# Cosine attention into a hard-swish MLP: the attention output of two pairs through one transposing DMA

## The chip, the cores and the metric

One core of a Trainium2 chip. The time is device microseconds of one execution of the program; a kernel's time is the median over its runs. In the text and in the profile PE is the matmul engine (PEld its weight loads), DVE the vector engine, ACT the scalar engine, POOL the general-purpose engine, and SP the engine that does nothing here but issue DMAs, one after another in program order.

## What is computed

Eight batches of twelve heads, 448 tokens, head dimension 64; the tokens then go through a two-layer MLP with a gated activation (768 to 2048 to 768). Inputs and output are float32.

```python
q_n = q / (np.linalg.norm(q, axis=-1, keepdims=True) + 1e-06)
k_n = k / (np.linalg.norm(k, axis=-1, keepdims=True) + 1e-06)
scores = np.matmul(q_n, k_n.transpose(0, 1, 3, 2)) / tau
attn = softmax(scores)                      # over the last axis
attn_out = np.matmul(attn, v)
x = attn_out.transpose(0, 2, 1, 3).reshape(B * S, H * D)      # 3584 x 768
h = x @ w_in
out = (h * np.clip(h + 3.0, 0.0, 6.0) / 6.0) @ w_out
```

## The kernel before

**Pairs and batches.** Two heads make a pair, so there are 48 pairs, numbered i = 0 to 47, six to a batch: pair i belongs to batch i // 6. For a pair, PE computes scores (L394), ACT their exponentials (L412), PE the product with v (L433), all in small groups; DVE then divides by the row sums and writes the pair's output as bf16 into a tile `on` of 128 x 512 (L448, L449, in `finish_values`). `on` has tokens on the partitions. The first matmul of the MLP needs the model dimension on the partitions, so `on` has to be transposed into `xT`: one 128 x 512 block of `xT[batch % 2]` for each pair.

**The way back.** For most of the first twelve pairs PE does this transpose (L466, L468) and DVE copies it out of PSUM (steps BK and CX). From pair 4 on, with few exceptions, SP does it with one transposing DMA of 128 x 512 elements (`back_crossbar`, L480, step XB): 42 of them. The tiles `on` come from a pool of three buffers, so the output of pair i can be written once the transpose of pair i - 3 has read its buffer.

**The MLP.** A batch's MLP starts when all its six pairs are in `xT`. It comes in units: `mm1_unit` (L496) is six matmuls of 448 columns over the six blocks of `xT`, block by block, so the k-th matmul reads the k-th pair of the batch; ACT (L505) and DVE (L511) turn its result into `gT`. `mm2_unit` (L532) is 16 matmuls over `gT` and ends in a copy (L543 on ACT or L545 on DVE) and two stores to the output (L553), which SP issues. The units of batch b are spread over the pairs of batch b + 1, so that PE always has matmuls beside the attention of the next pairs. Every engine works through its own list in program order.

**The order.** For the first 18 pairs the order of all steps is written out by hand in the strings of `PLAN`: two letters for the step, then the pair and other numbers. The steps that matter here: FI is `finish_values`, XB `back_crossbar`, VA the product with v, SC scores, EX exponentials, U one unit, UA and UV its work on ACT and DVE, LQ and LV loads of q or k and of v (issued on SP; L174 and L186), XD the transposing DMA of 128 x 896 elements that brings normalised q or k into place (L302, tile `tT`), CK and CS the copies of k (CS on POOL into `km`, L351), NM the normalising product (L246). From pair 18 on a loop (L682 to L722) gives the order. Its turn i does, in this order: SC i (three groups), EX i, VA i - 1, FI i - 1, the last group of SC and EX, then XB i - 1, for even i XD i + 2, one unit, some steps that prepare later pairs, one more unit, the other units of this turn, later preparations (for even i XD i + 3), LQ i + 7, for odd i LV, and VA i, group 0.

The first unit that reads a new batch b stands in turn i = 6 (b + 1) + 1, that is i = 19, 25, 31, 37, 43. The pair that completes the batch is transposed by the XB of the turn before. All DMA issues share SP's list with it: the loads, the stores (which wait for ACT's or DVE's copy) and the XDs.

Of the kernel before, what the change touches and what calls it, by code (L numbers as in the profile page):

```python
# [8 lines left out]
FP32 = mybir.dt.float32  # L9
BF16 = mybir.dt.bfloat16  # L10
AF = mybir.ActivationFunctionType
# [26 lines left out]
    "UA UA VA.7.0 EX.7.3 VA.7.1 UA CS.9.v UV W CS.8.v CK.8.v SC.8.0 UV UV SC.8.1 NM.10.p VA.7.2 VA.7.3 FI.7 EX.8.0",  # L38
    "SC.8.2 LQ.12 VC.8.p W EX.8.1 TR.10 U LV.5 EX.8.2 UA VA.8.0 CQ.11.v SC.8.3 SQ.13.p.0.7 VA.8.1 CQ.10.v UV",
    "SC.9.0 SC.9.1 EX.8.3 NM.11.p EX.9.0 RE.13 VA.8.2 SC.9.2 VA.8.3 FI.8 EX.9.1 SC.9.3 LQ.15 EX.9.2 U UA TR.11",  # L40
    "SQ.12.p.0.7 EX.9.3 RE.12 CS.11.v VA.9.0 VA.9.1 VC.10.p U CK.10.v XB.6 NO.6 NM.12.p VC.11.p SQ.15.p.0.7",
    "CK.11.v SC.10.0 CS.10.v UV VA.9.2 U UA SC.10.1 EX.10.0 UV UA EX.10.1 SC.10.2 VA.9.3 EX.10.2 LV.6 U UV UA",
    "TR.12 LQ.17 LQ.16 CQ.12.v XB.7 SC.10.3 U SQ.14.p.0.7 NM.13.p UV CQ.13.v SC.11.0 UA RE.15 FI.9 EX.10.3 EX.11.0",
    "U U UV UA UA VA.10.0 SC.11.1 EX.11.1 UV SC.11.2 EX.11.2 VA.10.1 UV VA.10.2 TR.13 SC.11.3 LQ.19 U LV.7 CS.12.a",
    "UA VA.10.3 RE.14 NO.7 SQ.17.p.0.7 NM.15.p CS.13.v CK.13.a U U FI.10 EX.11.3 UA VA.11.0 VA.11.1 VA.11.2",
    "NM.14.p SQ.16.a.0.7 UA CK.12.v SC.12.0 RE.17 XB.8 UV W U VA.11.3 VC.12.p U UV UV EX.12.0 FI.11 SC.12.1 UA",
    "XB.9 UV VC.15.p UA UV EX.12.1 LQ.18 SC.12.2 XB.10 VA.12.0 BK.11 SC.12.3 SC.13.0 EX.12.2 CX.11.v VA.12.1 XD.15",
    "U EX.12.3 EX.13.0 SC.13.1 SC.13.2 UA W U EX.13.1 VA.12.2 RE.16 SQ.19.p.0.7 VC.13.a VA.12.3 EX.13.2 UV SC.13.3",
    "UA U XD.14 FI.12 NO.8 UV SQ.18.p.0.7 CK.14.v U U EX.13.3 U VA.13.0 UA UV SC.14.0 UA UA UA EX.14.0 UV CS.14.v",
    "VC.14.a UV UV SC.14.1 EX.14.1 U SC.14.2 UA NM.16.v RE.19 UV EX.14.2 VA.13.1 U UA U W VA.13.2 UA RE.18 UV UV",  # L50
    "CK.15.v U LQ.20 SC.14.3 UA NO.9 XD.16 UV LQ.21 VA.13.3 U FI.13 U U NM.17.p XD.17 XB.13 UA VA.14.0 UV VA.14.1",
    "SC.15.0 UA EX.14.3 XB.12 VA.14.2 LV.8 UV UA UV EX.15.0 VA.14.3 SC.15.1 W EX.15.1 SC.15.2 FI.14 SQ.21.a.0.7",
    "CK.16.v EX.15.2 SC.15.3 SQ.20.a.0.2 U EX.15.3 U VA.15.0 SQ.20.p.2.5 VA.15.1 NM.19.v RE.20 UV SC.16.0 VC.17.v",
    "CS.16.v SC.16.1 UA CK.17.v SC.16.2 XD.19 EX.16.0 VC.16.v VA.15.2 RE.21 LQ.22 VA.15.3 U EX.16.1 EX.16.2",
    "SC.16.3 FI.15 UA NM.18.p U UV U XD.18 EX.16.3 UA NO.10 VA.16.0 VA.16.1 SC.17.0 SQ.22.p.0.7 SC.17.1 LV.9",
    "VC.18.p UV CK.18.v RE.22 EX.17.0 SC.17.2 VA.16.2 NM.20.v LV.11 XB.14 EX.17.1 VA.16.3 U LQ.23 VC.19.a SC.17.3",
    "UA U EX.17.2 FI.16 XB.16 UV CK.19.v LV.10 CS.18.v EX.17.3 VA.17.0 XB.15",
]


# [1 line left out]
def kernel(  # L62
# [10 lines left out]
    nc = tc.nc  # L73
    B, H, S, D = q.shape
# [3 lines left out]
    HP = H // 2  # L78
    NP = B * HP
# [11 lines left out]
    const = ctx.enter_context(tc.tile_pool(name="const", bufs=1))  # L91
    sb = ctx.enter_context(tc.tile_pool(name="sb", bufs=2))
# [8 lines left out]
    xT = [const.tile([128, CC, 512], BF16, name=f"xT{i}", tag=f"xT{i}") for i in range(2)]  # L101
# [21 lines left out]
        [const.tile([128, 2, 14], FP32, name=f"{x}{i}", tag=f"{x}{i}") for x in ("ln", "nr", "le", "r")]  # L123
        for i in range(2)
    ]
    eps_bias = const.tile([128, 1], FP32, name="eps_bias", tag="eps_bias")
    half_bias = const.tile([128, 1], FP32, name="half_bias", tag="half_bias")
    ident = const.tile([128, 128], BF16, name="ident", tag="ident")

    PV = psum.tile([128, 2, 512], FP32, name="PV", tag="PV")  # L130
# [11 lines left out]
    issued = set()  # L142

    def needs(*what):
        for w in what:
            assert w in issued or any(x < 0 for x in w[1:] if isinstance(x, int)), w
# [76 lines left out]
    def norms(d, *items):  # L223

        needs(("NM", 2 * d - 4), ("NM", 2 * d - 3))
        items = items or (0, 1)
        for x in items:
            needs(("RE", 2 * d + x))
        it = slice(items[0], items[-1] + 1)
        ln, nr, le, r = (t[:, it, :] for t in rs[d % 2])  # L230
        nc.scalar.activation(out=ln, in_=n2s[d % 2][:, it, :], func=AF.Ln)
        nc.scalar.activation(out=nr, in_=ln, func=AF.Exp, scale=0.5)
        nc.scalar.activation(out=le, in_=nr, func=AF.Ln, bias=eps_bias[:, :])
        nc.scalar.activation(out=r, in_=le, func=AF.Exp, scale=-1.0)  # L234
        for x in items:
            issued.add(("NO", d, x))
# [184 lines left out]
    def values(i, g):  # L421
# [4 lines left out]
        for n, name in enumerate(GROUPS[g]):  # L426
            for j in range(4):
# [11 lines left out]
                    skip_group_check=True,  # L439
                )  # L440

    def finish_values(i):
        needs(*(("VA", i, g) for g in range(4)), ("BK", i - 3))
        rc = sb.tile([128, 2, 4], FP32, name="rc", tag="rc", bufs=2)
        on = sb.tile([128, 4, 2, D], BF16, name="on", tag="on", bufs=3)
        on_of[i] = on
        pv4 = PV[:, :, 0:260].rearrange("p b (n e) -> p b n e", e=D + 1)
        nc.vector.reciprocal(out=rc[:, :, :], in_=pv4[:, :, :, D])  # L448
        nc.vector.tensor_tensor(  # L449
            out=on[:, :, :, :].rearrange("p (b j) h d -> p b (j h) d", b=2),  # L450
            in0=pv4[:, :, :, 0:D],
            in1=rc[:, :, :].to_broadcast([128, 2, 4, D]),
            op=ALU.mult,
        )
# [29 lines left out]
        issued.update((("BK", i), ("CX", i)))  # L484


    evac_n = [0]
    post = {"a": [], "v": []}

    def mm1_unit(b, fc):  # L490
        needs(*(("CX", i) for i in range(b * HP, (b + 1) * HP)))
        assert len(weights) <= 6 - 2 * (2 * fc // FCN)
        x, g, c0 = xT[b % 2], gT[(b // 2) % 2], (b % 2) * S
        ps, key = bank_of(None, 1)
        for cc in range(CC):
            nc.tensor.matmul(  # L496
                ps[:, 0:S],
                w_in_sb[:, cc, fc * 128 : (fc + 1) * 128],
                x[:, cc, 0:S],
                start=(cc == 0),  # L500
                stop=(cc == CC - 1),
            )
        def relu():
            u = sb.tile([128, S], BF16, name="u", tag="u", bufs=3)
            nc.scalar.activation(  # L505
                out=u[:, :], in_=ps[:, 0:S], func=AF.Relu, bias=half_bias[:, :], scale=1.0 / 6.0
            )
            post["v"].append(lambda: product(u))

        def product(u):  # L510
            nc.vector.scalar_tensor_tensor(  # L511
                out=g[:, fc, c0 : c0 + S],
                in0=u[:, :],
                scalar=1.0,
                in1=ps[:, 0:S],
                op0=ALU.min,
                op1=ALU.mult,
            )
            unread[key] = 0

        post["a"].append(relu)

    def mm2_unit(b, t, m, end=None):
# [97 lines left out]
    def whole_units(n):  # L621
# [5 lines left out]

    OPS = {
        "LQ": load_qk, "LV": load_v, "W": next_weights, "SQ": square, "RE": reduce, "NO": norms,
        "NM": normalise, "VC": vcast, "TR": transposes, "XD": crossbar, "XB": back_crossbar, "CQ": copy_q, "CK": copy_k, "CS": copy_k3, "SC": scores,  # L630
        "EX": exps, "VA": values, "FI": finish_values, "BK": back, "CX": copy_x, "U": unit, "UA": lambda: finish_units("a"), "UV": lambda: finish_units("v"),
        "UU": whole_units, "D": busy, "DP": busy_pv, "OPEN": open_ring,
    }
# [1 line left out]
    def do(op, *args):  # L635
        OPS[op](*args)
        key = (op,) + tuple(a for a in args if isinstance(a, int))
        if op not in ("RE", "NM", "LQ"):
            issued.add(key[:3] if op == "SC" else key)
# [42 lines left out]
    for i in range(FIRST, NP):  # L682
        n_u = len(units[i])
        even = i % 2 == 0

        def prepare(*what):
            for op, n, *args in what:
                if n < (NP // 2 if op in ("NO", "LV") else NP):
                    do(op, n, *args)

        for g in range(3):
            do("SC", i, g)
        for g in range(3):
            do("EX", i, g)
        for g in range(1, 4):
            if ("VA", i - 1, g) not in issued:
                do("VA", i - 1, g)
        do("FI", i - 1)
        do("SC", i, 3)
        do("EX", i, 3)  # L700

        do("XB", i - 1)
        if even:
            prepare(("XD", i + 2))
        do("UU", 1)
        if not even:
            prepare(("CS", i + 1))
        prepare(("SQ", i + 5, "p", 0, 7))
        n = 2
        do("UU", n - 1)  # L710
        if not even:
            prepare(("CK", i + 1), ("CK", i + 2))
        if not even:
            prepare(("NO", (i + 3) // 2))
        do("UU", n_u - n)
        prepare(("NM", i + 3, "p"), ("VC", i + 2, "p"), ("RE", i + 5))
        if even:
            prepare(("XD", i + 3))
        prepare(("LQ", i + 7))
        if not even:  # L720
            prepare(("LV", (i + 5) // 2))
        do("VA", i, 0)  # L722
# [1 line left out]
    do("VA", NP - 1, 2)  # L724
    do("VA", NP - 1, 3)
    do("FI", NP - 1)
    do("XB", NP - 1)
    do("UU", len(units[NP]))
    do("UU", len(stream))

# [34 lines left out]
```

## Time and profile before

| | us |
|---|---|
| median of 4 runs (lowest to highest) | 427.31 (426.56 to 428.82) |
| the profiled execution, its own time | 427.19 |
| its span in the profile | 425.4 |

| engine | busy, share of the span |
|---|---|
| PE (matmuls) | 97% |
| PEld (weight loads) | 57% |
| ACT | 64% |
| DVE | 51% |
| POOL | 43% |
| queue that SP feeds, share of 16 DMA engines | 61.6% |

The profile is of one execution. "Span" runs from its first to its last instruction. A line of a timeline gives the start, the length, the engine and the source line, what is written and read, and in square brackets how long the engine had stood idle before it and what ended that. SPq is SP's list: a line there is the issue of a DMA, not the transfer. The time from issue to landing is given apart: 3.9 us in the median for the 42 transposes `xT<-on`, from 2.4 to 15.1, and 3.0 for the 34 transposes `tT<-nrm`.

The DMA queues are fullest in the first quarter of the span, while the MLP's weights are loaded. PE's clock is reported in tenths of full speed; only one of the 40 equal slices of the span shows less than 9.

### The profile page before, as it was taken

The numbers are of one execution on the slowest core, as the hardware profiler recorded it, in microseconds if no ns is written. First come the engines' busy times: TensorE is split into PE (matmuls) and PEld (weight loads), VectorE is DVE, ScalarE is ACT, GpSimd is POOL, SyncE is SP. The second block draws the span as 40 slices with busy tenths as digits, with TensorE's granted clock in tenths as the row PEclk, the third lists the DMA queues.
The fourth block names the chain that finished last, engine by engine and source line by source line (L and its number), as shares of the span: only waits on it lengthen the run. The fifth ranks groups of instructions, "written<-read, shape, count | busy, mean of one in ns | idle before, by whom it ended". The sixth has DMA issues, their size and how long they took to land.

```text
span 425.4 us, 9252 instructions
## 1 busy us (share of the span) xinstructions
PE 413.4 (97%) x3575; PEld 243.6 (57%) x3575; DVE 218.1 (51%) x419; ACT 271.3 (64%) x593; POOL 181.3 (43%) x184
## 2 busy tenths in 40 slices
PE   6999999999997999999999999999999999999996
PEld 5556655555663555555555555655555655655564
DVE  7689777666433454554555554455554344215410
ACT  6999989966554775676765775676675675105400
POOL 5997787412234464374373373373471310000000
PEclk9999999999998999999999999999999999999999
DMA  8998999997878669767889867667667251230033
GB/s 292 304 237 207 237 198 208 192 179 190 199 175 188 172 157 159 171 167 163 152 201 151 155 161 168 151 171 182 156 159 104 56 80 33 64 80 19 2 75 76
DMA packets 94156, 65.82 MB, mean 155 GB/s; under 512 B 58656, under 2 KB 92576, under 8 KB 94112
## 3 DMA queue, kind: packets, MB, share of 16 engines
q1 hardware_dynamic: 90320, 58.89, 61.6%
q0 software_dynamic: 3712, 6.29, 9.1%
q8 instruction: 28, 0.46, 0.5%
q14 instruction: 16, 0.13, 0.1%
q10 hardware_dynamic: 80, 0.05, 0.0%
HBM read 47.19 MB, written 11.01 MB: 137 GB/s over the span
## 4 chain that ended last, share of the span: by engine, by line
PE 78%; DMA 11%; ACT 3%; DVE 3%; SPq 1%; POOL 1%; issue 1%; POOLq 0%; ACTq 0%; DVEq 0%
PE M L532 23%; PE M L496 18%; PE PV L433 9%; PE Y L532 6%; DMA raw<-in_q_dram 5%; PE Z L532 5%; PE Y L496 5%; PE M L394 5%; PE Z L496 4%; DMA tT<-nrm 2%; ACT at L412 2%; DMA vr<-in_v_dram 2%; PE Z L394 1%; PE SC L394 1%; SPq L186 1%; DVE n L215 1%
## 5 line engine op out<-in xcount | busy, mean ns | idle before, releaser
L532 PEld LDWEIGHTS <-gT 128*128 128x128 bf16 x912 | 88.8, 98 | 59.1 <-issue 0.4
L412 ACT ACTIVATE at<-M 128x448 bf16<-128x448 f32 x195 | 94.9, 567 | 30.0 <-PE M L394 25.3
L496 PEld LDWEIGHTS <-w_in_sb 128*128 128x128 bf16 x768 | 74.6, 98 | 68.6 <-issue 5.5
L532 PE MATMUL M<-w_out_sb,gT 128*128 128x384 bf16 (+1 forms) x640 | 106.2, 322 | 0.0
L496 PE MATMUL M<-xT,w_in_sb 128*128 128x448 bf16 x510 | 105.9, 356 | 0.2 <-DVE gT L511 0.2
L246 POOL TENSOR_TENSOR nrm<-raw,r 128x896 bf16<-128x896 f32 (+1 forms) x45 | 74.2, 1655 | 24.7 <-ACT r L234 21.0
L203 POOL TENSOR_TENSOR sq<-raw 128x896 f32<-128x896 f32 (+3 forms) x42 | 67.8, 1618 | 27.6 <-DMA raw<-in_k_dram 11.0
L511 DVE SCALAR_TENSOR_TENSOR gT<-u,M 128x448 bf16<-128x448 bf16 x85 | 52.4, 620 | 50.7 <-ACT u L505 49.5
L505 ACT ACTIVATE u<-M,half_bias 128x448 bf16<-128x448 f32 x85 | 55.1, 651 | 22.2 <-PE M L496 20.7
L433 PEld LDWEIGHTS <-at 128*128 128x128 bf16 x1344 | 53.3, 98 | 25.7 <-issue 18.5
L433 PE MATMUL PV<-vx,at 128*128 128x65 bf16 (+1 forms) x1344 | 63.9, 198 | 0.0
L215 DVE TENSOR_REDUCE n<-sq 128x14 f32<-128x896 f32 (+1 forms) x50 | 51.9, 1040 | 3.2 <-ACT sq L201 2.4
L351 POOL COPY km<-tT 64x128 bf16<-64x128 bf16 x34 | 10.6, 312 | 100.0 <-DMA tT<-nrm 50.8
L543 ACT COPY o<-M 128x384 f32<-128x384 f32 (+1 forms) x21 | 9.9, 471 | 42.0 <-PE M L532 42.0
L394 PE MATMUL M<-tT,kz 64*128 64x448 bf16 (+1 forms) x172 | 34.0, 353 | 1.3 <-DVE o L545 0.5
L449 DVE TENSOR_TENSOR on<-PV,rc 128x512 bf16<-128x512 f32 x48 | 33.2, 692 | 3.6 <-DMA xT<-on 1.9
L545 DVE COPY o<-M 128x384 f32<-128x384 f32 (+1 forms) x19 | 10.4, 547 | 47.3 <-PE M L532 46.0
L412 ACT ACTIVATE at<-Y 128x448 bf16<-128x448 f32 x48 | 27.4, 571 | 9.7 <-PE Z L394 9.7
L412 ACT ACTIVATE at<-Z 128x448 bf16<-128x448 f32 x51 | 28.9, 567 | 3.1 <-PE M L394 2.7
L496 PE MATMUL Y<-xT,w_in_sb 128*128 128x448 bf16 x138 | 29.9, 353 | 0.0
L448 DVE RECIPROCAL rc<-PV 128x8 f32<-128x8 f32 x48 | 9.9, 206 | 37.6 <-PE PV L433 34.3
L496 PE MATMUL Z<-xT,w_in_sb 128*128 128x448 bf16 x120 | 26.1, 353 | 2.2 <-DMA xT<-on 2.2
(78 smaller groups left out, 343.5 us busy)
## 6 DMA issues: line engine op xcount, KB each, us to landing
vr<-in_v_dram SPq DMA_DIRECT2D x96, 128.0 KB, 4.0
raw<-in_k_dram SPq DMA_DIRECT2D x24, 448.0 KB, 4.4
raw<-in_q_dram SPq DMA_DIRECT2D x24, 448.0 KB, 4.8
out_dram<-o SPq DMA_DIRECT2D x110, 96.0 KB, 2.2
w_in_sb<-in_moe_w_in_dram POOLq DMA_DIRECT2D x4, 768.0 KB, 12.2
w_out_sb<-in_moe_w_out_dram POOLq DMA_DIRECT2D x4, 768.0 KB, 12.3
xT<-on SPq DMA_TRANSPOSE x42, 3.9
tT<-nrm SPq DMA_TRANSPOSE x34, 3.0
```

The source lines that it names most:

```text
L203: engines[e].tensor_tensor(out=o, in0=i, in1=i, op=ALU.mult)
L215: nc.vector.tensor_reduce(out=n2s[d % 2][:, j % 2, c], in_=sq[:, :, :, :].rearrange("p g c d -> p (g c) d")[:, c, :], axis=AX.X, op=ALU.add,)
L246: engines[e].tensor_tensor(out=nrm[:, :, g, :].rearrange("p c g d -> p g c d"), in0=raw_of[j][:, g, :, :], in1=rs[d % 2][3][:, j % 2, :] . ...
L351: nc.gpsimd.tensor_copy(out=km[p, :, p], in_=z[p, 3, :, :])
L394: nc.tensor.matmul(o, ks, qt[rows], start=True, stop=True)
L412: nc.scalar.activation(out=o, in_=x, func=AF.Exp, scale=inv_tau)
L433: nc.tensor.matmul(o, at[:, n, q_cols(i // HP, j)], mv, start=(name == "A0" and j % 2 == 0), stop=last, skip_group_check=True,)
L449: nc.vector.tensor_tensor(out=on[:, :, :, :].rearrange("p (b j) h d -> p b (j h) d", b=2), in0=pv4[:, :, :, 0:D], in1=rc[:, :, :].to_broad ...
L496: nc.tensor.matmul(ps[:, 0:S], w_in_sb[:, cc, fc * 128 : (fc + 1) * 128], x[:, cc, 0:S], start=(cc == 0), stop=(cc == CC - 1),)
L505: nc.scalar.activation(out=u[:, :], in_=ps[:, 0:S], func=AF.Relu, bias=half_bias[:, :], scale=1.0 / 6.0)
L511: nc.vector.scalar_tensor_tensor(out=g[:, fc, c0 : c0 + S], in0=u[:, :], scalar=1.0, in1=ps[:, 0:S], op0=ALU.min, op1=ALU.mult,)
L532: nc.tensor.matmul(ps[:, 0:width], lhs, w_out_sb[:, fc, cols], start=(fc == 0), stop=(fc == FCN - 1),)
```

## The change

A new step XP, `back_two(i)`, for even i: one transposing DMA of 128 x 1024 elements for the pairs i and i + 1 together. Both write their output into the two halves of one tile `on` of 128 x 1024, of which there are now two buffers in place of three of half the size. The tile is taken by the even pair, in `finish_values`; this pair waits until the pairs i - 4 and i - 3 have been transposed.

In the loop, XP i - 2 stands in the turns with even i, where XB i - 1 stood; the XB of odd turns are gone. In `PLAN`, XP.6, XP.8 and XP.12 stand about where the second of their two XB stood, XP.14 where XB.15 stood at the plan's end; XB.6, XB.8, XB.13 and the early XB.14 are gone, and XB.16 too, since the pairs 16 and 17 are done by the loop's XP 16 in turn 18. Pairs 4 and 10, whose neighbours 5 and 11 go back through PE, keep an XB of their own, from their half of the shared tile. All in all 42 transposing DMAs become 20 double and 2 single ones. The other steps keep their order. Two constants of one column (`eps_bias`, `half_bias`) move into one tile of two columns.

```diff
@@ PLAN (the lines that lose or gain a step, cut to those steps)
-    ... XB.6 NO.6 NM.12.p ...
+    ... NO.6 NM.12.p ...
-    ... CQ.12.v XB.7 SC.10.3 ...
+    ... CQ.12.v XP.6 SC.10.3 ...
-    ... RE.17 XB.8 UV W ... SC.12.1 UA
-    XB.9 UV VC.15.p ... SC.12.2 XB.10 VA.12.0 BK.11 ...
+    ... RE.17 UV W ... SC.12.1 UA XP.8 UV VC.15.p
+    ... SC.12.2 XB.10 VA.12.0 BK.11 ...
-    ... XD.17 XB.13 UA VA.14.0 ... EX.14.3 XB.12 VA.14.2 ...
+    ... XD.17 UA VA.14.0 ... EX.14.3 XP.12 VA.14.2 ...
-    ... LV.11 XB.14 EX.17.1 ... FI.16 XB.16 UV ... LV.10 CS.18.v EX.17.3 VA.17.0 XB.15
+    ... LV.11 EX.17.1 ... FI.16 UV ... LV.10 CS.18.v EX.17.3 VA.17.0 XP.14
@@
-    eps_bias = const.tile([128, 1], FP32, name="eps_bias", tag="eps_bias")
-    half_bias = const.tile([128, 1], FP32, name="half_bias", tag="half_bias")
+    bias = const.tile([128, 2], FP32, name="bias", tag="bias")
+    eps_bias, half_bias = bias[:, 0:1], bias[:, 1:2]
@@
+    twin_on = {}
+
     def finish_values(i):
-        needs(*(("VA", i, g) for g in range(4)), ("BK", i - 3))
+        needs(*(("VA", i, g) for g in range(4)))
+        if i % 2 == 0:
+            needs(("BK", i - 4), ("BK", i - 3))
+            twin_on[i // 2] = sb.tile([128, 2, 4, 2, D], BF16, name="on", tag="on", bufs=2)
         rc = sb.tile([128, 2, 4], FP32, name="rc", tag="rc", bufs=2)
-        on = sb.tile([128, 4, 2, D], BF16, name="on", tag="on", bufs=3)
+        on = twin_on[i // 2][:, i % 2, :, :, :]
@@
+    def back_two(i):
+        needs(("FI", i), ("FI", i + 1))
+        assert i % 2 == 0
+        b, hp = i // HP, i % HP
+        del on_of[i], on_of[i + 1]
+        nc.sync.dma_start_transpose(
+            out=xT[b % 2][:, hp : hp + 2, :].rearrange("p a (j n) -> p (a j) n", j=4),
+            in_=twin_on[i // 2][:, :, :, :, :].rearrange("p a j h d -> p (a j h d)"),
+        )
+        for x in (i, i + 1):
+            issued.update((("BK", x), ("CX", x)))
@@ the loop over i
-        do("XB", i - 1)
+        if even:
+            do("XP", i - 2)
         if even:
             prepare(("XD", i + 2))
@@ after the loop
-    do("XB", NP - 1)
+    do("XP", NP - 2)
```

## The prediction

> **What bounds the kernel now.** I read the page first (engine shares, then the chain that ended last), then what PE waited for, then SP's timeline around that wait, and last fine windows of clock and DMA. The page says that PE is the bound, and the view of waits that next to none of its time is waiting once the start is over:
>
> ```profile
> PE 413.4 (97%) x3575; PEld 243.6 (57%) x3575; DVE 218.1 (51%) x419; ACT 271.3 (64%) x593; POOL 181.3 (43%) x184
> ...
> PE Z L496 <- DMA xT<-on: 2.2, 1, 2.2
> ```
>
> The second line is the one wait on exactly the transfer that the change touches. The chain of waits around it (start, length, what):
>
> ```profile
> 117.94 2.27 PE M L496 x12
> 120.21 5.20 PE M L532 x32
> 126.53 4.01 DMA xT<-on
> 130.93 3.88 PE M L496 x12
> 134.82 2.67 PE M L532 x16
> ```
>
> Twelve L496 matmuls take 2.27 us before the wait and 3.88 after it. The windows say why (the last three columns are PE clock, DMA share, GB/s):
>
> ```profile
> 129.50:130.00 0.50, 0.00 (x0) 0.00 (x0) 0.00 (x0) 0.00 (x0) 0.00 (x0) 1.00 1.35 217
> ...
> 132.00:132.50 0.50, 0.50 (x3) 0.28 (x2) 0.26 (x1) 0.00 (x0) 0.42 (x2) 0.50 0.54 141
> ```
>
> PE stands still, then runs at half clock until 134.5. The waited-for transfer is pair 17's (the loop's XB at i = 18), the last that batch 2's first L496 unit needs. It was issued late for lack of room on SP, not for lack of data. SP's timeline:
>
> ```profile
> 115.56 1.28 SPq L480 DMA_TRANSPOSE xT<-on  x1
> 116.89 0.59 SPq L174 DMA_DIRECT2D raw<-in_q_dram  x1
> 117.57 1.61 SPq L553 DMA_DIRECT2D out_dram<-o  x2
> 119.28 1.22 SPq L480 DMA_TRANSPOSE xT<-on  x1
> 120.60 1.17 SPq L553 DMA_DIRECT2D out_dram<-o  x2
> 121.82 2.66 SPq L186 DMA_DIRECT2D vr<-in_v_dram  x4
> 124.52 1.28 SPq L480 DMA_TRANSPOSE xT<-on  x1
> 125.85 0.58 SPq L174 DMA_DIRECT2D raw<-in_k_dram  x1
> 126.53 1.21 SPq L480 DMA_TRANSPOSE xT<-on  x1
> ```
>
> SP issues back to back here. The four L480 lines are pairs 14, 16, 15, 17. DVE wrote pair 17's output at 119.94 to 120.63, 5.9 us before its issue; and even that write had stood 1.94 us, until pair 14's transfer freed its buffer.
>
> [...] clock 0.50 for some 3.4 us after a stop of 2.4. [...] The trace has one nearly alone:
>
> ```profile
> 350.00:350.50 0.50, 0.50 (x5) 0.24 (x3) 0.00 (x0) 0.50 (x2) 0.00 (x0) 1.00 0.25 54
> 350.50:351.00 0.50, 0.50 (x4) 0.25 (x3) 0.30 (x1) 0.50 (x2) 0.00 (x0) 1.00 0.98 202
> 351.00:351.50 0.50, 0.50 (x4) 0.29 (x3) 0.50 (x2) 0.29 (x1) 0.00 (x0) 1.00 0.06 7
> ```
>
> Shares 0.25 + 0.98 + 0.06 by 0.5 us are 0.65 us of all engines; I use 0.65. [...]
>
> **The change part by part.**
>
> *SP.* 42 transposes become 22 (20 double ones, pairs 4 and 10 alone). An issue costs 1.21 us for 512 columns and 1.25 for the 896 of L302, so I take 1.26 for 1024; the bounds are 1.2 and 2.4 (twice 1.21). In the stretch above, the issues of pairs 14 and 16 alone go: 116.89 - 115.56 and 120.60 - 119.28, 2.65 us. What stands between was ready earlier (the stored tiles by 115.1 and 116.5, pair 15 by 115.1). So the last transfer goes out at 126.53 - 2.65 = 123.88. The wait of pair 17's output write for pair 14's buffer goes too: its slot was last read by pairs 12 and 13, landed before 100. In the later loops SP waits for stored tiles that PE sets, so the freed issues there advance nothing.
>
> *The wait at batch 2.* Before: the sixth matmul at 130.58 instead of 127.25 + 5 x 0.19 = 128.20, so 2.38; the slow clock adds 3.88 - 2.27 = 1.61 and 0.07 in the next group: 4.06 us in all. After: landing took 4.01, plus 0.65 for the second half: 128.54. The double transfer ahead of it (pairs 14 and 15) adds 0.65 more if nothing hides it; the DMA share of 122 to 126 is mostly 0.3 to 0.9, so I take it as hidden, and keep 0.65 for the range. Pair 16 is now late as well, so the fifth matmul waits, at 128.01. Stop: 0.5 us (0 to 1.2). A stop that short leaves the clock: PE stood for about 0.6 us between 100 and 102 at clock 1.00. Gain 4.06 - 0.5 = 3.56.
>
> *The other batch borders (first use at i = 25, 31, 37, 43).* The double transfer stands where the odd one stood, lands 0.65 later, and is needed one matmul (0.19) earlier. i = 25: 176.04 + 3.7 + 0.65 = 180.39, needed 179.51 + 0.76 = 180.27: 0.1 us late. i = 31: 221.65 + 5.3 + 0.65 = 227.6, needed 228.5: nothing. i = 43: 317.52 + 2.6, needed after 324: nothing. i = 37 has no slack today:
>
> ```profile
> 273.54 1.23 SPq L480 DMA_TRANSPOSE xT<-on  x1
> ...
> 275.96 2.51 PE L496 MATMUL M<-xT,w_in_sb 128*128 128x448 bf16 x12
> ...
> 276.98 1.99 PEld L496 LDWEIGHTS <-w_in_sb 128*128 128x128 bf16 x11 [0.17 <-issue]
> ```
>
> The landing at 276.94 already holds a weight load by 0.17 (0.08 of PE). After: 277.59 against 276.72, 0.87, so 0.8 more. Bounds for these borders together: 0.3 and 5.
>
> *The rest, at nothing.* The first batches: batch 1's first L496 runs at 73.05; pair 10 landed at 70.9, pairs 8 and 9 by 68.5; 0.65 more is covered, with 2 us to spare. FI of an even pair now waits for the transfer of the pairs three and four back, issued two loop turns earlier: covered by some 8 us a turn. What queues behind that wait on DVE is the gT products and copies that free PSUM banks, so a miss would reach PE. The L302 transpose right behind each double one lands up to 0.65 later; its reader is POOL's copy of km, which waits anyway with POOL busy 43%. The tile shared by the two biases changes no instruction's shape.
>
> **Sum.** -3.56 + 0.1 + 0.8 = -2.66. The profiled execution took 427.19 (its span 425.4), so 424.5; the median is 0.12 above it: 424.6.
>
> **The rivals.**
>
> *Slower: the double transfer is held up in flight.* DMA sometimes stops almost wholly while a transpose is under way: from 224.6 to 226.2 hardly a byte moves, and pair 29's transfer took 5.3 us to land instead of about 3.5; the issue behind an L302 transpose took 2.38 at 341.58 and 3.02 at 325.64 instead of 1.21. A double transfer [...] has an L302 transpose pushed in behind it at once. If each lands 6 us after its issue (7.3 at i = 31), the stops are 123.88 + 6 - 128.01 = 1.9, 1.8 at i = 25, 0.4 at i = 31 and 2.8 at i = 37, 6.9 in all, with slow clock (1.6 each) at one to three of them: 8.5 to 11.7, less 4.06, so about 432. It decides once the stops together cost over 6.2 us, that is from landings some 1.5 us above mine. Against it: at 333.24 a single one with L302 right behind landed in 2.4.
>
> *No change: the stop shrinks too little.* If XP.16 lands at 129.5, PE still stands 1.5 us and the clock may fall all the same; then 1.5 + 1.68 + 0.9 = 4.1 against 4.06: 427.3. For it: no trace shows the shortest stop that halves the clock.
>
> *It isn't early at all.* If SP waits elsewhere for the 2.65 us, the border costs 0.65 + 0.19 more, 428.9 with the others; the timeline shows no such wait. I count it with the case of no change.
>
> **How the numbers follow.** 0.5%, 2.1 us, is about what a measurement of this kernel can tell from no change: 425.2 and 429.4 are the edges. Forecast 0.56 (own range 423 to 425.9), no change 0.18, slower 0.26. A tenth of the forecast's weight lies above 425.2: faster 0.51, same 0.22, slower 0.27. The low end is the whole 4.06 gained with little lost, 423.0; the high end cuts into the slower case at 430.5.
>
> **What would show it.** Right: SP's last double transpose before batch 2 issued near 124; PE's wait there under 1.2 us, clock 1.00 throughout 131 to 135; a wait of about 0.9 us at i = 37; double transposes issuing in about 1.26 us. Wrong: issues near 2.4 us, landings of 6 us in the loop, waits of L496 for xT at several borders, or clock 0.50 at any of them.

## The result, and the profile after

The changed kernel takes 424.79 us in the median of 37 runs (423.28 to 428.83); the kernel before, run beside it on the same chips, takes 427.27. The ratio is 0.9949, with a 95% interval of 0.9933 to 0.9966: about 2.2 us faster, and the whole interval lies below 1. The ratio leaves out the few executions that were over 1.5% slower than the fastest of their kernel, so it is not that of the two medians. The profiled execution took 424.61, its span is 422.8 (before: 427.19 and 425.4).

On the page, PE's busy time is all but the same, and there are about half as many transposes of the attention output. Over all of them the time from issue to landing is as before (3.8 in the last column, 3.9 before); place by place it is longer, as the last section shows:

```profile
PE 412.7 (98%) x3575; PEld 243.9 (58%) x3575; DVE 218.3 (52%) x419; ACT 271.2 (64%) x593; POOL 181.3 (43%) x184
...
xT<-on SPq DMA_TRANSPOSE x22, 3.8
```

The view of waits has PE's wait for this transfer down from 2.2 us to 0.6 (total, times, longest); `mm1_unit` is L513 now:

```profile
PE Z L513 <- DMA xT<-on: 0.6, 1, 0.6
```

SP's timeline ahead of it (start, length; L497 is `back_two`, L570 the stores):

```profile
118.98 3.21 SPq L186 DMA_DIRECT2D vr<-in_v_dram  x4
122.23 1.34 SPq L497 DMA_TRANSPOSE xT<-on  x1
123.61 0.57 SPq L174 DMA_DIRECT2D raw<-in_k_dram  x1
124.29 1.23 SPq L497 DMA_TRANSPOSE xT<-on  x1
125.62 1.65 SPq L302 DMA_TRANSPOSE tT<-nrm  x1
127.36 2.47 SPq L570 DMA_DIRECT2D out_dram<-o  x4
129.93 1.26 SPq L302 DMA_TRANSPOSE tT<-nrm  x1
```

The same row stands as before, with two issues fewer. The last transfer for batch 2 goes out at 124.29 instead of 126.53, and everything behind it moves up. The timeline of PE at that place before the change,

```profile
127.25 1.11 PE L496 MATMUL Z<-xT,w_in_sb 128*128 128x448 bf16 x5
130.58 0.35 PE L496 MATMUL Z<-xT,w_in_sb 128*128 128x448 bf16 x1 [2.22 <-DMA xT<-on]
130.77 4.04 PE L496 MATMUL M<-xT,w_in_sb 128*128 128x448 bf16 x12
134.61 2.88 PE L532 MATMUL M<-w_out_sb,gT 128*128 128x384 bf16 x16
137.32 0.41 PE L433 MATMUL PV<-vx,at 128*128 128x65 bf16 x8
```

and after it:

```profile
127.22 0.92 PE L513 MATMUL Z<-xT,w_in_sb 128*128 128x448 bf16 x4
128.71 0.54 PE L513 MATMUL Z<-xT,w_in_sb 128*128 128x448 bf16 x2 [0.57 <-DMA xT<-on]
129.09 2.43 PE L513 MATMUL M<-xT,w_in_sb 128*128 128x448 bf16 x12
131.36 2.76 PE L549 MATMUL M<-w_out_sb,gT 128*128 128x384 bf16 x16
133.96 0.41 PE L433 MATMUL PV<-vx,at 128*128 128x65 bf16 x8
134.53 0.35 PE L394 MATMUL M<-tT,kz 64*128 64x448 bf16 x1 [0.17 <-DMA tT<-nrm]
```

Four matmuls run, then the fifth and sixth wait together, for pairs 16 and 17 come in one transfer. The stop is 0.57 us, and the twelve after it take 2.43 us, at clock 1.00. From the first L513 to the next group of L433 it is 133.96 - 127.22 = 6.74 us; from L496 before it was 137.32 - 127.25 = 10.07. The last line shows who is late next: a forward transpose, by 0.17. The chain of waits has the same news; two of its rows, 125.62 and 129.93, are the forward transposes (start, length):

```profile
125.62 3.90 DMA tT<-nrm
129.93 4.47 DMA tT<-nrm
```

Where before had `xT<-on` in this place, after has `tT<-nrm`. At the batch borders of i = 25 and i = 37 the timeline of PE shows

```profile
176.38 1.57 PE L513 MATMUL Y<-xT,w_in_sb 128*128 128x448 bf16 x6
...
273.11 2.47 PE L513 MATMUL M<-xT,w_in_sb 128*128 128x448 bf16 x12
```

Six matmuls took 1.57 instead of 1.30: 0.27 lost to a transfer issued at 172.91 that landed at 177.41. Twelve took 2.47, against 2.43 undisturbed: nothing to speak of at i = 37.

### The profile page after: what moved, and what is told of

It reads as the page before. It is cut to its first block, busy times and chain, and to the rows that moved or that the text cites. A ratio compares the mean times of both kernels' runs of the same rounds, so it can differ in the third digit from the quotient of the medians.

```text
span 422.8 us, 9195 instructions
## 1 busy us (share of the span) xinstructions
PE 412.7 (98%) x3575; PEld 243.9 (58%) x3575; DVE 218.3 (52%) x419; ACT 271.2 (64%) x593; POOL 181.3 (43%) x184
## 4 chain that ended last, share of the span: by engine, by line
PE 82%; DMA 8%; ACT 4%; SPq 4%; issue 1%; DVE 1%; POOL 1%; ACTq 0%; POOLq 0%
PE M L513 21%; PE M L549 20%; PE PV L433 10%; PE Y L513 5%; PE M L394 5%; PE Y L549 5%; PE Z L549 5%; PE Z L513 5%; DMA tT<-nrm 5%; ACT at L412 3%; PE Z L394 1%; DMA raw<-in_k_dram 1%; SPq L186 1%; PE SC L394 1%; DMA xT<-on 1%; PE Y L394 1%
## 5 line engine op out<-in xcount | busy, mean ns | idle before, releaser
L513 PEld LDWEIGHTS <-w_in_sb 128*128 128x128 bf16 x768 | 74.2, 98 | 66.6 <-issue 2.8
L513 PE MATMUL M<-xT,w_in_sb 128*128 128x448 bf16 x510 | 104.2, 353 | 0.2 <-DVE gT L528 0.2
L246 POOL TENSOR_TENSOR nrm<-raw,r 128x896 bf16<-128x896 f32 (+1 forms) x45 | 74.2, 1655 | 23.4 <-ACT r L234 19.7
L522 ACT ACTIVATE u<-M,bias 128x448 bf16<-128x448 f32 x85 | 55.1, 652 | 21.3 <-PE M L513 20.0
L433 PEld LDWEIGHTS <-at 128*128 128x128 bf16 x1344 | 53.3, 98 | 24.9 <-issue 17.7
L433 PE MATMUL PV<-vx,at 128*128 128x65 bf16 (+1 forms) x1344 | 64.0, 198 | 0.0
L513 PE MATMUL Y<-xT,w_in_sb 128*128 128x448 bf16 x138 | 30.0, 352 | 0.1
L513 PE MATMUL Z<-xT,w_in_sb 128*128 128x448 bf16 x120 | 26.1, 353 | 0.6 <-DMA xT<-on 0.6
```

Source lines behind the costliest of these rows:

```text
L246: engines[e].tensor_tensor(out=nrm[:, :, g, :].rearrange("p c g d -> p g c d"), in0=raw_of[j][:, g, :, :], in1=rs[d % 2][3][:, j % 2, :] . ...
L433: nc.tensor.matmul(o, at[:, n, q_cols(i // HP, j)], mv, start=(name == "A0" and j % 2 == 0), stop=last, skip_group_check=True,)
L513: nc.tensor.matmul(ps[:, 0:S], w_in_sb[:, cc, fc * 128 : (fc + 1) * 128], x[:, cc, 0:S], start=(cc == 0), stop=(cc == CC - 1),)
L522: nc.scalar.activation(out=u[:, :], in_=ps[:, 0:S], func=AF.Relu, bias=half_bias, scale=1.0 / 6.0)
```

## The experiments

Three theories. A: the gain is SP's room in the 10 us ahead of batch 2's first unit, nothing else. B: it is the buffer of `on` that comes free earlier, so that pair 17's output is written at once. C: fewer and larger transfers are cheaper all along the kernel. In all ratios below the kernel before was run beside the experiment on the same chip; its medians lay between 426.41 and 427.69.

**Buffers alone.** The kernel before with a fourth buffer (and the shared bias tile, which makes room for it):

```diff
-        needs(*(("VA", i, g) for g in range(4)), ("BK", i - 3))
+        needs(*(("VA", i, g) for g in range(4)), ("BK", i - 4))
-        on = sb.tile([128, 4, 2, D], BF16, name="on", tag="on", bufs=3)
+        on = sb.tile([128, 4, 2, D], BF16, name="on", tag="on", bufs=4)
```

> Single transposes as before, but four buffers for the pairs' outputs in place of three, so that pair 17's output no longer waits for pair 14's transfer. Theory A (the gain is SP's room ahead of batch 2's first unit): SP reaches pair 17's transfer at the same 126.5 us, PE still waits 2.2 us there and runs at half clock after it, 427.3 us. Theory B (the gain is the freed buffer wait): no stop at batch 2, about 424.8. Theory C (fewer and larger transfers all along): 427.3.

Measured 426.41, ratio 1.0002 (0.9977 to 1.0026). The stop is all there (timeline of PE):

```profile
131.50 0.53 PE L496 MATMUL Z<-xT,w_in_sb 128*128 128x448 bf16 x1 [2.37 <-DMA xT<-on]
131.82 3.92 PE L496 MATMUL M<-xT,w_in_sb 128*128 128x448 bf16 x12
```

B falls: pair 17's output was written by 119.5 and had its turn on SP only at 127.62.

**Doubles in the plan only, and in the loop only.** The changed kernel with single transposes from pair 18 on; then the reverse, with the plan of before and doubles from pair 18 on. The loop's line in the first of the two:

```diff
-        if even:
-            do("XP", i - 2)
+        if i == FIRST:
+            do("XP", i - 2)
+        else:
+            do("XB", i - 1)
```

> Double transposes only up to pairs 16 and 17; from pair 18 on single ones, from the halves of the shared tile. Theory A: the stop at batch 2 stays at about 0.6 us with full clock, and the 0.3 us at batch 3 goes, 424.5. Theory C: most of the doubles are gone, so most of the gain, about 426.8. Theory B: 424.8.

> Single transposes up to pair 17, double ones from pairs 18 and 19 on; the shared tiles are there from the start. Theory A: pair 17 is issued at 126.5 as before, the stop of 2.2 us and the half clock are back, and 0.3 at batch 3 is added: 427.5. Theory B: the buffer wait is gone, about 424.8. Theory C: 18 of 20 double transfers remain, about 425.

Plan only: 423.93, ratio 0.9942 (0.9907 to 0.9978), as good as the whole change. Its last double transfer goes out at 123.30 and the stop is 0.49. Loop only: 428.91, ratio 1.0038 (1.0015 to 1.0062), slower than before. Its timeline of PE has the stop of before, and one more behind it:

```profile
130.18 0.35 PE L513 MATMUL Z<-xT,w_in_sb 128*128 128x448 bf16 x1 [2.14 <-DMA xT<-on]
130.37 2.43 PE L513 MATMUL M<-xT,w_in_sb 128*128 128x448 bf16 x12
...
136.41 0.35 PE L394 MATMUL M<-tT,kz 64*128 64x448 bf16 x1 [0.77 <-DMA tT<-nrm]
```

So the whole gain comes from the pairs up to 17, and the 15 doubles behind them (15, not the 18 that the expectation counts) bring none. C falls. (The profiled execution of loop only took 426.32, less than the median; that its twelve matmuls take 2.43 us, at clock 1.00, after a stop of 2.14 us comes up again below.)

**The issues put back.** The changed kernel with the single transposes of pairs 14 and 16 issued again at their old places, ahead of the double ones, which write the same data a second time:

```diff
-    ... NM.20.v LV.11 EX.17.1 ... FI.16 UV ...
+    ... NM.20.v LV.11 XA.14 EX.17.1 ... FI.16 XA.16 UV ...
+    def again(i):
+        b, hp = i // HP, i % HP
+        nc.sync.dma_start_transpose(
+            out=xT[b % 2][:, hp, :].rearrange("p (j n) -> p j n", j=4),
+            in_=on_of[i][:, :, :, :].rearrange("p j h d -> p (j h d)"),
+        )
```

> The changed kernel, and two single transposes of pairs 14 and 16 issued as well where they stood before (the same data goes into xT twice). Theory A: SP loses 2.65 us again, the double transfer of 16 and 17 goes out at 126.9 and lands near 131.3; PE stops some 3.2 us and runs at half clock after it: 424.8 + 2.7 + 1.6, about 429. Theories B and C: the buffers and the large transfers are all there, 424.8 to 425.2.

Measured 430.17, ratio 1.0084 (1.0047 to 1.0121). SP issues the last double one at 127.92 instead of 124.29, and the timeline of PE (L520 is `mm1_unit` here) reads

```profile
128.20 0.54 PE L520 MATMUL Z<-xT,w_in_sb 128*128 128x448 bf16 x2
129.27 0.54 PE L520 MATMUL Z<-xT,w_in_sb 128*128 128x448 bf16 x2 [0.53 <-DMA xT<-on]
132.49 0.93 PE L520 MATMUL Z<-xT,w_in_sb 128*128 128x448 bf16 x2 [2.68 <-DMA xT<-on]
133.21 3.60 PE L520 MATMUL M<-xT,w_in_sb 128*128 128x448 bf16 x12
```

Two issues of 1.2 us put back, and the stop (2.68 us) and the half clock (0.50 from 132.2 to 135.6) are back, with a second stop of 0.53 us for pairs 14 and 15. The double transfer is there, the gain is not.

**One issue only.** The plan of before, in which only the pairs 14 and 15 go back together; the other transfers up to pair 17 stay single. From pair 18 on doubles as in the change.

> As the changed kernel from pair 18 on; of the hand-written part only pairs 14 and 15 go back together, so SP gains one issue, 1.33 us, ahead of pair 17's single transfer. Theory A: it goes out near 125.2, lands near 129.2, and the sixth matmul waits about 1.0 us. If a stop of 1 us leaves the clock alone, about 424.9; if it halves the clock as well, about 426.5.

Measured 425.55, ratio 0.9972 (0.9953 to 0.9992): 1.2 us (0.3 to 2.0), about half the gain for half the room. The last transfer goes out at 125.12, PE stands 1.38 us, and the next twelve matmuls take 2.43, as at clock 1.00 in the changed kernel; at i = 37 PE stands another 0.94 us for `xT`.

**The room without the doubles, first try.** The kernel before with the raw load of v for the pairs 20 and 21 (LV.10, four issues, 2.66 us) behind the XB of turn 18:

```diff
-    ... UV CK.19.v LV.10 CS.18.v ...
+    ... UV CK.19.v CS.18.v ...
         do("XB", i - 1)
+        if i == FIRST:
+            do("LV", 10)
```

> The kernel before, single transposes and three buffers; only the four loads of LV.10 (2.66 us of SP) are issued right behind pair 17's transpose instead of ahead of pair 15's. Theory A: pair 17 goes out at about 123.9, lands by 128, PE does not stop and its clock stays at 1.00: 427.3 less 4.06, about 423.3. Theories B and C: nothing that they name has changed, 427.3.

Measured 426.76, ratio 1.0005 (0.9979 to 1.0031): the expectation of A missed. The stop at batch 2 is gone (its six L496 take 1.39 us), but the load is now ahead of the two forward transposes, which go out at 129.47 and 133.39, and at the next scores the timeline of PE has

```profile
136.70 0.35 PE L394 MATMUL M<-tT,kz 64*128 64x448 bf16 x1 [1.97 <-DMA tT<-nrm]
```

The hole has moved to the next piece of work that SP's list delays. In this execution 4.0 us are won at the one place (6.09 for the stretch of 10.07) and 2.0 lost at the other; that the ratio shows nothing of the rest goes with the clock: 11 of the 14 executions had a mean clock of 0.996 or less, the profiled one 1.0. Where they lost it is not shown.

**Second try.** The load behind both forward transposes, at the end of turn 18, and with it GpSimd's cast of v for pair 20, so that the order of load and cast stays (LV.10 leaves the plan as in the first try):

```diff
-        prepare(("NM", i + 3, "p"), ("VC", i + 2, "p"), ("RE", i + 5))
+        prepare(("NM", i + 3, "p"))
+        if i > FIRST:
+            prepare(("VC", i + 2, "p"))
+        prepare(("RE", i + 5))
         if even:
             prepare(("XD", i + 3))
+        if i == FIRST:
+            prepare(("LV", 10), ("VC", 20, "p"))
```

> The kernel before, all transposes single, three buffers; LV.10 (2.66 us of SP) and POOL's cast of pair 20 that needs it stand at the end of turn 18, behind both L302 transposes of that turn and not only behind pair 17's transpose. Theory A in its wider form (SP's room ahead of batch 2's first unit and of the next pairs' L302 transposes): pair 17 out near 124, the second L302 transpose near 129 instead of 131.75, no stop at either place, the gain of the change without any double transfer, 2.5 to 3.5 us under the kernel before. If doubling itself is what helps, no gain.

Measured 427.62, ratio 0.9989 (0.9958 to 1.0021): missed again. No stop for `xT` or `tT` any more; the hole has moved to GpSimd. Its timeline has

```profile
137.17 0.61 POOL L265 CAST vx<-vr 128x512 bf16<-128x512 f32 x1 [12.25 <-DMA vr<-in_v_dram]
137.72 0.64 POOL L351 COPY km<-tT 64x128 bf16<-64x128 bf16 x2
```

and PE's timeline

```profile
138.42 0.36 PE L394 MATMUL M<-tT,km 128*128 128x448 bf16 x1 [2.96 <-POOL km L351]
138.62 1.30 PE L496 MATMUL Y<-xT,w_in_sb 128*128 128x448 bf16 x6
```

GpSimd had stood 12.25 us before a cast that waited for the late load, and the copies to `km` came behind it in its list: they start at 137.72, and PE waits 2.96 us for them. The same move on the other two kernels,

> Double transposes up to pairs 16 and 17 only, single ones in the loop, and LV.10 with its cast at the end of turn 18. Theory A: the double transfer goes out near 121.7, the stop of 0.5 us at batch 2 goes as well, 0.5 us under the run with doubles in the hand-written part only; about 423.4.

> The changed kernel, and LV.10 with its cast at the end of turn 18. Theory A: no stop at batch 2 any more (0.57 before) and none at pair 20's scores (0.17); batch 3's 0.27 stays; about 0.6 us under the changed kernel, 424.1.

gave 425.03 (ratio 0.9940, 0.9905 to 0.9975) with a wait of 1.2 us for `km`, and 425.85 (0.9951, 0.9929 to 0.9974) with waits of 1.1 us for ACT's exponentials and 0.7 us for `xT` at another border: no better than without the move, and both expectations missed. A milder move on the changed kernel, all loads of v behind the next turn's XP,

> The changed kernel, with the loads of v moved behind the next turn's double transpose in SP's list (LV.10, and those of all later odd turns). Theory A: batch 2's transfer goes out near 121.7 and batch 3's 2.7 us earlier; neither stop is left (0.57 and 0.27 us), 424.0. If v then comes late for its cast and product, a new wait of PE on POOL's or DVE's cast takes the gain back: 425 or more.

gave 424.67, ratio 0.9944 (0.9923 to 0.9965): the waits of L513 for `xT` are gone, but the time is that of the changed kernel (0.9949). Its trace has 1.2 us of waiting for GpSimd's `nrm` (L246), which is no price of the move: it lies before 65 us, and the first moved load goes out at 123.64.

**Third try.** The load stands as in the second try; the cast goes one turn further, behind the copies to `km`, directly ahead of the cast of pair 21 that needs the same load:

```diff
-            prepare(("LV", 10), ("VC", 20, "p"))
+            prepare(("LV", 10))
         prepare(("NM", i + 3, "p"))
+        if i == FIRST + 1:
+            prepare(("VC", 20, "p"))
         if i > FIRST:
             prepare(("VC", i + 2, "p"))
```

> The kernel before, with one raw load of v (the pair of loads for heads 20 and 21) issued only at the end of turn 18, behind its last forward transpose, and GpSimd's cast that needs it for pair 20 moved to turn 19, directly ahead of the cast of pair 21, so that GpSimd's copies of k no longer stand behind a wait for that load. Nothing is doubled. If only SP's room ahead of batch 2's first unit counts (theory A): no wait for xT at batch 2, for tT at pair 20 or for km at pair 20, and 2.0 to 3.5 us less than before, so as good as the change. If the larger transfer itself helps (theory C): within 1 us of before. If each hole is only followed by the next late piece: within 1 us of before too, with a new wait of 1 us or more in the stretch from 128 to 145 us, which the trace would name.

> Doubles of the pairs up to 17 alone, singles after it, with the same move of the raw load and of the cast. Theory A: the 0.5 us stop at batch 2's first unit goes, so at most 0.5 us below the kernel with the doubles up to pair 17 alone, 2.5 to 4 us below before. If the next late piece takes it: no better than that kernel, with a wait of its own in the stretch from 128 to 145 us.

The kernel before with this move alone, every transfer single: 423.64, ratio 0.9918 (0.9888 to 0.9948). SP's timeline and PE's:

```profile
122.92 1.20 SPq L480 DMA_TRANSPOSE xT<-on  x1
124.22 1.24 SPq L302 DMA_TRANSPOSE tT<-nrm  x1
125.55 2.46 SPq L553 DMA_DIRECT2D out_dram<-o  x4
128.12 1.26 SPq L302 DMA_TRANSPOSE tT<-nrm  x1
129.43 3.42 SPq L186 DMA_DIRECT2D vr<-in_v_dram  x4
```

```profile
125.89 1.30 PE L496 MATMUL Z<-xT,w_in_sb 128*128 128x448 bf16 x6
127.03 2.43 PE L496 MATMUL M<-xT,w_in_sb 128*128 128x448 bf16 x12
129.30 2.76 PE L532 MATMUL M<-w_out_sb,gT 128*128 128x384 bf16 x16
131.90 0.41 PE L433 MATMUL PV<-vx,at 128*128 128x65 bf16 x8
```

The last transfer goes out 126 - 123 = 3 us ahead of the unit, and the stretch that took 10.07 us before and 6.74 in the changed kernel takes 131.90 - 125.89 = 6.01: no stop at all. (The next group then waits 0.39 us for a copy on ACT.) Nothing is doubled, and the gain, 3.5 us by the ratio (2.2 to 4.8), is no smaller than that of the change (1.5 to 2.9 by its interval). That is theory A by itself.

With the doubles up to pair 17 as well: 422.84, ratio 0.9899 (0.9871 to 0.9926), the best of all. Its interval lies below that of the change (0.9933 to 0.9966), but not below those of the move alone or of the doubles up to pair 17 alone, so that the two together are more than each is not shown.

## Why the prediction was right, and where its terms were off

It gave 424.6 us; 424.79 was measured. By its steps:

- *SP's room.* Right. 123.88 was forecast for the last transfer, 124.29 measured: the two issues are gone, but the load of v in between took 3.21 instead of 2.66. Pair 17's output no longer waits for a buffer (1.94 us before), and FI's new wait, put at nothing, does not show. That these two issues are the cause is shown from both ends: put back, the loss is back; made elsewhere, without any doubling, the gain is there.
- *The issue price.* Right: 1.26 taken, 1.28 in the median of the 20 double ones.
- *Landing and stop.* 4.66 us to land was forecast, 4.4 measured, so the late issue and the quicker landing nearly cancel: a stop of 0.57 where 0.5 was forecast. The clock stayed at 1.00 (in every half microsecond from 127 to 137), and pair 16's half waited for pair 17's, as the forecast had assumed: the fifth and sixth matmul run together at 128.71, behind the 0.57. The gain in this stretch is 10.07 - 6.74 = 3.33, against 3.56.
- *The other borders.* 0.1 was forecast at i = 25 and 0.27 came; nothing at i = 31 and i = 43, right. At i = 37 the 0.8 did not come in this trace: SP issued the transfer 273.11 - 270.04 = 3.07 us ahead of the unit, before only 275.96 - 273.54 = 2.42, because a raw load ahead of it had then taken 1.64 us instead of 0.59. But that was luck. Four other kernels with doubles in the loop wait there: 0.36 (loop only), 0.51 (issues put back), 0.94 (one issue) and 0.75 (second try on the changed kernel). With single ones there the most is 0.28 (buffers alone). The forecast had the mechanism right; how often the changed kernel pays is not shown by one trace. Loop only is slower than before by 1.6 us (0.6 to 2.6) by its ratio; how much of that is the doubles' late landing is not separated.
- *What is late next.* Put at nothing: the prediction named GpSimd's copy of `km` as the reader of the transpose behind the double one, but PE's scores read `tT` too. For pair 20 they wait: 0.17 of idle PE and 0.23 in all. A later start of its transpose turns it into the main wait, as the first try showed: issued at 133.39, it held PE for 1.97.

The sum for PE: 3.33 - 0.23 - 0.27 = 2.83; its last row starts at 410.79 instead of 413.66, 2.87 earlier. What follows PE's end is 0.3 longer, so the span is 2.6 shorter, where 2.66 was forecast. The terms were off by up to 0.8 either way and cancel; that the sum fits to 0.1 is luck.

One term is less firm than its place in the sum suggests. The half clock (1.68 us of the 4.06) is there in the profiled execution of before, but not in each. Half clock for 3.4 us (0.50 from 131.4 to 134.8) lowers the mean clock over 425 us by 0.004, to 0.996. Of the 158 executions of before that the experiments' ratios use, 83 had a mean clock of 0.996 or less (median 427.79), the other 75 more (median 426.18). Of the changed kernel's 38 only 6 had 0.996 or less; the median of the other 32 is 424.64. At the higher clock the two kernels are thus 426.18 - 424.64 = 1.5 us apart, about what the stop lost (2.22 - 0.57). The rarer half clock adds, by an estimate from these figures, (83/158 - 6/38) x (427.79 - 426.18) = 0.6 us. Together that is the measured 2.2. A mean clock does not say where the clock was lost, but the shares go with the stop: 14 of 20 in loop only, 7 of 9 with the issues put back and 8 of 22 with the buffers alone, against 1 of 9 in plan only and none of 15 in the third try without doubles.

Of the rivals, the slower one did not come: at the later batch borders one transfer took 6.3 us to land, at i = 31, where it has room; the others took 3.5 to 4.5. What it rests on is there in small: double transfers did land later, by 0.6 us in the median (last section). Nor did the two cases of no change come: the issue was early, and the stop was 0.57.

## What to carry to other kernels

Where one engine issues all DMAs and issues back to back, as SP does here, look at the place of the awaited transfer in its list (with two issues fewer ahead of it, it went out at 124.29 instead of 126.53): count the issues ahead of it, and take away or move any that nobody waits for. Before making the transfers larger, try the order alone; here it gave no less. Moving an issue back only pays if every reader of it is looked at, in order, on each engine: in the kernel before, the three tries with the same load gave nothing that could be measured, the same again, and 3.5 us, and the last two differ only in the place of one cast.

## What the runs showed of the hardware

*The clock and the length of a stop.* The length of the stop alone does not decide the clock here. After stops of 2.22 us (before), 2.37 (buffers alone) and 2.68 (issues put back) it was at 0.50 for 3.4 us; after 2.14 (loop only) and 2.96 (second try) it stayed at 1.00. In the best kernel's profiled execution it was at 0.50 for 3.4 us (84.5 to 87.9) after four stops, none over 1 us and 1.46 in all:

```profile
82.15 0.36 PE L394 MATMUL Z<-tT,kz 64*128 64x448 bf16 x1 [0.93 <-DVE kz L341]
...
82.67 0.35 PE L394 MATMUL M<-tT,kz 64*128 64x448 bf16 x1 [0.16 <-DVE gT L528]
83.20 0.35 PE L394 MATMUL M<-tT,kz 64*128 64x448 bf16 x1 [0.18 <-DVE gT L528]
83.73 1.74 PE L513 MATMUL M<-xT,w_in_sb 128*128 128x448 bf16 x6 [0.19 <-DVE gT L528]
```

Idle time alone does not decide it either: 2.96 us in one piece left the clock at 1.00, and 1.46 in four pieces came ahead of 0.50. What decides it stays open; no run here shifted a stop of fixed length to test it.

*A transposing DMA cost SP nearly the same at both sizes:* 1.23 us in the median for 512 columns (before), 1.28 for 1024 (after). It is the landing that shows the second half. The medians over all transfers hide this (3.9 and 3.8). From pair 14 on, each double transfer can be set against the single one of its odd pair in the kernel before: 15 of the 17 took longer, by 0.6 us in the median, and the five that are awaited at i = 19, 25, 31, 37 and 43 by 0.4, 0.8, 1.0, 0.4 and 0.9. The prediction's 0.65, from the share of the engines that one transpose took, is of that size.

*Pauses of the DMA engines.* In the kernel before nothing at all moves from 225.0 to 225.5 (windows view; the last two columns are the share of the 16 engines and GB/s), with a transfer `xT<-on` in flight:

```profile
225.00:225.50 0.50, 0.50 (x5) 0.30 (x4) 0.00 (x0) 0.00 (x0) 0.00 (x0) 1.00 0.00 0
225.50:226.00 0.50, 0.50 (x11) 0.37 (x9) 0.04 (x1) 0.00 (x0) 0.00 (x0) 1.00 0.08 9
```

The transfer, issued at 221.65, took 5.3 us to land. There are more such pauses in the same trace, with under 10 GB/s in each half microsecond, from 165.0 to 167.0 and from 342.0 to 343.5. What makes them was not tried.
